# ScalarE's two copies of the last half-product, and its two transfers of the block before it, change places

## The chip, the cores and the metric

The kernel runs on one core of a Trainium2 chip. The metric is the time of one execution on the device in microseconds (us). Four executions of the kernel before gave 875.29, 875.60, 875.69 and 1138.22 us; their median is 875.64. A profile of one further execution shows where that time goes, instruction by instruction.

## The reference

The program is an attention block followed by a feed-forward block. Only the second one matters here:

```python
def _attn_ref(q, k, v, proj) -> np.ndarray:   # q, k, v: (4, 8, 768, 64)
...
    scores = np.where(mask, scores, -1000000000.0)
...
    return np.matmul(attn, v).astype(np.float32)
...
def _moe_ref(x, w_in, w_out) -> np.ndarray:   # x: (3072, 512), w_in: (512, 2048), w_out: (2048, 512)
    h = x @ w_in
    g = h * (1.0 / (1.0 + np.exp(-1.702 * h)))
    return (g @ w_out).astype(np.float32)
```

The attention output, reordered to 3072 tokens of 512 values, is `x`. The output is 3072 x 512 float32, which is 6.3 MB.

## The kernel before

After attention, `feed_forward` (L683) computes both products by Strassen's scheme in Winograd's form: a product of 2 x 2 blocks is made of seven block products and a few sums. The second product, `g @ w_out`, uses the scheme twice. Its outer level has seven "outer products", run in the order `OUTER = (1, 2, 6, 7, 5, 3, 4)` (L692), for each of three blocks of 1024 tokens (`n1`, L688). That gives 21 steps in `steps_out` (L772), numbered `n` = 0 to 20; the loop over them stands at L922. A block of 1024 tokens has two halves of 512 tokens, `j` = 0 and 1, which are collected in the tiles `ys[0]` and `ys[1]`. I call the last one y1 where it is `ys[1]` of the last block.

Each step calls `product_of_halves` (L813), the inner level. It makes seven inner products with TensorE, each by four matrix products of 128 x 128 by 128 x 256 in float32 into a PSUM bank of its own (`product(i)`, L821; the trace shows eight matmul instructions for each). I write P1, P3 and so on for `product(1)`, `product(3)`. The sums around them run on VectorE, all through `add` (L827, recorded at L828). Two results leave PSUM through ScalarE: the copy of P1 into `u` (L837) and the copy of P3 into `c12` (L840). The next VectorE sum, `add(v, product(6), u)` (L842), reads `u`.

The four quadrants of a step's result are turned from feature-major to token-major by VectorE's 32 x 32 transposes (`turned`, L799, recorded at L804), one instruction for each quadrant, into `ys[j]`. `written` (L806) then sends a part of `ys[j]` to the output in DRAM, as four transfers of 32 partitions each, dealt in turn to the queues it is given. In the steady part all four go to SyncE's queue (SP). For the last two steps they are dealt to SP and to ScalarE's queue alternately (`loader + [nc.scalar]`), so two each. A transfer that sits in ScalarE's instruction stream waits there, in order, until the transposes that fill its source are done.

The order of TensorE, VectorE, ScalarE and GpSimd is the order of the Python calls: these four are in `ORDERED` (L18) and are scheduled by hand (L72). `after(at)` (L934) is a hook called at five points of `product_of_halves`; it places the prepared sums of the next step, the transposes and the transfers between the inner products. Its arguments 0, 1, 2, 3 stand for points of L841, L849, L853 and L858, and 4, which only the last step reaches, for L856.

Around the change the order is:

- Step 19 (`n + 2 == len(steps_out)`, outer product 3) ends with `after(3)`. That places the rest of the sums for step 20 and the four transposes of its own result into y1, and at L951 and L952 `written(sb, 1, (0, 1), ...)`: four transfers of 256 KB, two on SP and two on ScalarE.
- Step 20 (`final`, outer product 4) starts with the ScalarE copies of P1 and P3. Its products run in the order P1, P3, P6, P7, P5, P2, P4. Its `after(2)` transposes quadrants 1 and 3 and sends the second half of `ys[0]` (four transfers of 128 KB). Its `after(4)` transposes quadrant 0, and `after(3)` quadrant 2, and sends the first half (four transfers of 128 KB).

So at the end 1 MB of y1 leaves first, then 0.5 MB, then 0.5 MB, each as two transfers on SP's queue and two on ScalarE's.

Of the kernel before, what the change touches and what calls it, by code (L numbers as in the profile page):

```python
# [38 lines left out]
def kernel(  # L39
# [643 lines left out]
    def feed_forward(tag, late=()):  # L683
# [9 lines left out]
        with ExitStack() as fctx:  # L693
# [71 lines left out]
            def inner_sums(at):  # L765

                if at == 0:
                    w = w_quarters(OUTER[0])
                    return sums_a(nc.gpsimd, *w, wqs[LEFT[OUTER[0]]][:, 1, 0:F4, :])
                return sums_a(nc.gpsimd, *w_quarters(OUTER[at])) if at < len(OUTER) else []  # L770

            steps_out = [(sb, o) for sb in range(n1) for o in OUTER]  # L772
            raw_g = [None, s_in[:, 0:2].rearrange("p i k f -> p (i k f)").rearrange("p (c t) -> p c t", t=XT)]

            def fetch(n):
                sb, o = steps_out[n]
                for h in range(2):
                    cs = slice(h * F4, (h + 1) * F4)
                    loader[0].dma_start(out=raw_g[n % 2][:, cs], in_=g_dram[len(LEFT) * sb + RIGHT[o], :, cs, :])
# [14 lines left out]
            def g_sums(n):  # L794
                return sums_b(nc.vector, *g_quarters(n)) if n < len(steps_out) else [lambda: None] * 4
# [3 lines left out]
            def turned(c, i, j, q0, q1):  # L799

                for q in range(q0, q1):
                    h, k = divmod(q, 2)
                    y = ys[j].rearrange("p b (d r) -> p r b d", r=4)[:, 2 * i + h, k * (TH // 32) : (k + 1) * (TH // 32), :]
                    nc.vector.transpose(y, c[:, q].rearrange("p (b t) -> p b t", t=32))  # L804

            def written(sb, j, halves, queues):  # L806
                first, last = halves[0] * TH, (halves[-1] + 1) * TH
                for a in range(4):
                    t0 = (2 * sb + j) * XT
                    dst = out[t0 + first : t0 + last, a * P : (a + 1) * P].rearrange("(b t) d -> t b d", t=32)  # L810
                    queues[a % len(queues)].dma_start(out=dst, in_=ys[j][32 * a : 32 * (a + 1), first // 32 : last // 32, :])

            def product_of_halves(n, acc, after):  # L813

                sb, o = steps_out[n]
                wq, gq = w_quarters(o), g_quarters(n)
                m = wholes[n % len(wholes)]
                u, v = (gp.tile([P, TH], F32, tag=x, name=x, bufs=2) for x in ("u", "v"))
                c11, c12, c21, c22 = (m[:, i] for i in range(4))

                def product(i):  # L821
                    ps = bank()[:, 0:TH]
                    for c in range(F4):
                        nc.tensor.matmul(ps, wq[LEFT[i]][:, c, :], gq[RIGHT[i]][:, c, :], start=(c == 0), stop=(c == F4 - 1))  # L824
                    return ps

                def add(dst, x, y):  # L827
                    nc.vector.tensor_tensor(dst, x, y, op=Alu.add)  # L828

                def corner():  # L830
                    add(c11, product(2), u)
                    if acc is not None:
                        add(c11, c11, acc[:, 0])


                final = n + 1 == len(steps_out)
                nc.scalar.copy(u, product(1))  # L837
                if not final:
                    corner()
                nc.scalar.copy(c12, product(3))  # L840
                after(0)  # L841
                add(v, product(6), u)  # L842
                add(c21, product(7), v)
                if acc is not None:
                    add(v, v, acc[:, 1])
                    add(c22, c21, acc[:, 3])
                    add(c21, c21, acc[:, 2])
                add(c12, c12, v)
                after(1)  # L849
                p = product(5)  # L850
                add(c22, p, c21 if acc is None else c22)
                add(c12, p, c12)
                after(2)  # L853
                if final:
                    corner()
                    after(4)  # L856
                add(c21, product(4), c21)
                after(3)  # L858
                return m
# [14 lines left out]
            for sb in range(n1):  # L874
                for mt in range(MT):
                    n = sb * MT + mt
# [45 lines left out]
            for n, (sb, o) in enumerate(steps_out):  # L922
                final = n + 1 == len(steps_out)
                if 0 < n and n + 1 < len(steps_out):
                    fetch(n + 1)

                if n in (5, 6):
                    nc.gpsimd.tensor_copy(mark, ms[OUTER[n - 1]][0:1, 0, 0:1])
                for f in {0: inner_sums(4), 5: inner_sums(5) + inner_sums(6)[:2], 6: inner_sums(6)[2:]}.get(n, []):
                    f()  # L930
                later_sums = g_sums(n + 1)
                m = wholes[n % len(wholes)]

                def after(at):  # L934
                    if at == 0:
                        while pending:
                            pending.pop(0)()

                    steps = [later_sums[at : at + 1]] if n == 0 else [[], later_sums[0:1], later_sums[1:2], later_sums[2:], []][at : at + 1]

                    if n + 2 >= len(steps_out):
                        turns = [lambda q=q: turned(m, int(final), int(not final), q, q + 1) for q in range(4)]
                        if final:
                            steps = [[[], [], [turns[1], turns[3]], [turns[2]], [turns[0]]][at]]
                        elif at == 3:
                            steps = [later_sums[2:3], turns[0:2], turns[3:4], later_sums[3:], turns[2:3]]
                    for f in sum(steps, []):
                        f()
                    if final and at in (2, 3):
                        written(sb, 0, (3 - at,), loader + [nc.scalar])  # L950
                    if n + 2 == len(steps_out) and at == 3:  # L951
                        written(sb, 1, (0, 1), loader + [nc.scalar])  # L952

                acc = {6: 1, 7: 6, 2: 1, 3: 6, 4: 7}.get(o)
                if o == 3:
                    pending.pop(0)()
                ms[o] = product_of_halves(n, None if acc is None else ms[acc], after)

                def flat(x):
                    return x.rearrange("p q t -> p (q t)")  # L960

                if o == 5:
                    m5, m6, m7 = (ms[i] for i in (5, 6, 7))
                    pending += [lambda a=m6, b=m5: nc.vector.tensor_tensor(flat(a), flat(a), flat(b), op=Alu.add),
                                lambda a=m5, b=m7: nc.vector.tensor_tensor(flat(a), flat(a), flat(b), op=Alu.add),
                                lambda a=m5: turned(a, 1, 1, 0, 4)]
                elif o in (2, 3) and n + 2 < len(steps_out):
                    pending.append(lambda a=ms[o], j=int(o == 3): turned(a, 0, j, 0, 4))
                    if o == 3:
                        pending.append(lambda sb=sb: written(sb, 1, (0, 1), loader))  # L970
                elif o == 4 and not final:
                    pending.append(lambda a=ms[4]: turned(a, 1, 0, 0, 4))
                    pending.append(lambda sb=sb: written(sb, 0, (0, 1), loader))
                yield
# [50 lines left out]
```

## Time and profile before

| what | value |
|---|---|
| median of the four runs | 875.64 us |
| the profiled execution's own time | 875.59 us |
| its span (first to last instruction) | 873.7 us |
| granted TensorE clock, mean | 0.996 |
| TensorE busy | 862.2 us (99%), 4077 matmuls |
| VectorE busy | 718.9 us (82%) |
| ScalarE busy | 311.8 us (36%) |
| DMA moved | 131.99 MB, mean 151 GB/s |
| output transfers of 256 KB, SP's queue / ScalarE's queue | 18 / 2 |
| output transfers of 128 KB, SP's queue / ScalarE's queue | 4 / 4 |

The span runs from the first to the last instruction of the program; the execution's own time is 1.89 us longer. Times inside the trace are counted from the start of the span. A timeline line gives the start, the duration, the engine (a "q" behind its name means its instruction queue, which issues transfers), the line of the kernel, the operation, the tiles written and read, and the number of instructions that the line merges. In square brackets stands how long the engine sat idle before it and what released it. Step 20 starts on TensorE at about 851.9 us; the last matmul of the program ends at 864.1, the last VectorE instruction at 866.2, and the span at 873.7.

### The profile page before, as it was taken

The page shows a single profiled execution, that of the slowest core. Times are in us where ns is not written, and L with a number is a line of the kernel's source. Part 1 is how long each engine was busy: PE and PEld are TensorE (multiplying, and loading weights), DVE is VectorE, ACT ScalarE, POOL GpSimd, SP SyncE. Part 2 cuts the span into 40 slices and gives each one's busy share as a digit, 9 for nine tenths or more (in the row PEclk, how much of TensorE's full clock was granted, in tenths as well). Part 3 has the DMA queues.
Part 4 walks back from the last instruction along what each step waited for, and adds up shares of the span by engine and source line. Part 5 has one row for each costly group of instructions (what it writes and reads, how often), then busy time and mean ns, then how long its engine had stood idle before and what let it go on. Part 6 is the DMA issues. An engine that isn't in the chain of part 4 may idle for free.

```text
span 873.7 us, 11818 instructions
## 1 busy us (share of the span) xinstructions
PE 862.2 (99%) x4077; PEld 501.3 (57%) x4077; DVE 718.9 (82%) x1020; ACT 311.8 (36%) x519; POOL 321.1 (37%) x275
## 2 busy tenths in 40 slices
PE   9999999999999999999999999999999999999995
PEld 4444444444444444444444444444888888888884
DVE  4479999988999988778777778888888977897785
ACT  5756667777666653222233222332000000000000
POOL 4244334334433375665543344659903100000000
PEclk9999999999999999999999999999999999999998
DMA  6334456554445404565455555575844685467524
GB/s 133 59 59 84 84 98 106 115 90 83 83 83 90 76 25 157 193 217 193 175 193 186 205 181 197 189 251 179 302 164 157 200 249 196 166 196 241 193 97 99
DMA packets 169155, 131.99 MB, mean 151 GB/s; under 512 B 123616, under 2 KB 138112, under 8 KB 163712
## 3 DMA queue, kind: packets, MB, share of 16 engines
q1 hardware_dynamic: 166528, 129.70, 51.4%
q10 hardware_dynamic: 2560, 1.46, 0.8%
q8 instruction: 34, 0.56, 0.3%
q14 instruction: 33, 0.27, 0.1%
HBM read 79.69 MB, written 50.33 MB: 149 GB/s over the span
## 4 chain that ended last, share of the span: by engine, by line
PE 96%; DVE 3%; issue 0%; ACT 0%; ACTq 0%; DVEq 0%
PE product L712 33%; PE product L824 27%; PE ps L432 18%; PE av L458 14%; PE dn L479 1%; PE hash L408 1%; DVE xT L828 1%; PE tp L366 1%; DVE y L804 1%; DVE acc L448 0%; DVE xT L499 0%; PE warm L359 0%; PE hash L373 0%; DVE acc L446 0%; ACT e L433 0%
## 5 line engine op out<-in xcount | busy, mean ns | idle before, releaser
L433 ACT ACTIVATE e<-ps 128x768 f32<-128x768 f32 x192 | 150.3, 812 | 17.1 <-PE ps L432 14.9
L432 PE MATMUL ps<-qT,kT 64*128 64x384 f32 x768 | 155.1, 482 | 0.0
L712 PE MATMUL product<-xT,w_in_sb 128*128 128x512 f32 x288 | 135.4, 592 | 0.0
L458 PE MATMUL av<-e,v 128*64 128x385 f32 x768 | 128.2, 488 | 0.0
L440 POOL TENSOR_TENSOR acc<-e 128x768 f32<-128x768 f32 x32 | 51.2, 1600 | 192.4 <-ACT e L433 112.6
L720 ACT ACTIVATE c<-c 128x512 f32<-128x512 f32 x72 | 45.3, 630 | 184.9 <-issue 78.5
L458 PEld LDWEIGHTS av<-e,v 128*64 128x64 f32 x768 | 53.8, 136 | 72.9 <-issue 72.0
L712 PEld LDWEIGHTS product<-xT,w_in_sb 128*128 128x128 f32 x288 | 54.6, 190 | 69.0 <-issue 63.8
L712 PE MATMUL product<-t_x,s_in 128*128 128x512 f32 x192 | 90.2, 592 | 0.0
L432 PEld LDWEIGHTS ps<-qT,kT 64*128 64x128 f32 x768 | 68.2, 187 | 37.7 <-issue 37.4
L219 POOL TENSOR_TENSOR v<-c,u 128x512 f32<-128x512 f32 x24 | 34.2, 1424 | 121.1 <-ACT c L720 121.1
L837 ACT COPY u<-product 128x256 f32<-128x256 f32 x21 | 7.8, 372 | 172.1 <-PE product L824 138.9
L441 POOL TENSOR_TENSOR acc<-acc,e 128x768 f32<-128x768 f32 x32 | 64.1, 2002 | 2.5
L432 PE MATMUL ps<-qf,kf 64*128 64x384 bf16 x384 | 63.0, 324 | 0.1
L712 PEld LDWEIGHTS product<-t_x,s_in 128*128 128x128 f32 x192 | 36.5, 190 | 45.9 <-issue 43.8
L446 DVE SCALAR_TENSOR_TENSOR acc<-e 128x768 f32<-128x768 f32 x32 | 50.6, 1582 | 5.1 <-ACT e L433 5.1
L712 PE MATMUL product<-t_x,w_in_sb 128*128 128x512 f32 x96 | 45.1, 592 | 0.0
L712 PE MATMUL product<-xT,s_in 128*128 128x512 f32 x96 | 45.1, 592 | 0.0
L432 PEld LDWEIGHTS <-kf 64*128 64x128 bf16 x384 | 19.4, 94 | 35.4 <-issue 12.0
L448 DVE TENSOR_TENSOR acc<-acc,acc 128x768 f32<-128x768 f32 x32 | 31.2, 974 | 4.8 <-POOL acc L441 1.6
L824 PE MATMUL product<-raw_g,xT 128*128 128x256 f32 x152 | 35.1, 379 | 0.0
L448 DVE TENSOR_TENSOR acc<-acc,e 128x768 f32<-128x768 f32 x32 | 31.8, 995 | 3.8 <-ACT e L433 0.5
(207 smaller groups left out, 1495.1 us busy)
## 6 DMA issues: line engine op xcount, KB each, us to landing
raw_g<-g_dram SPq DMA_DIRECT2D x22, 1024.0 KB
s_in<-g_dram SPq DMA_DIRECT2D x20, 1024.0 KB
g_dram<-c SPq DMA_DIRECT2D x72, 256.0 KB
g_dram<-t SPq DMA_DIRECT2D x48, 256.0 KB
raw<-in_moe_w_in_dram SPq DMA_DIRECT2D x16, 512.0 KB
raw<-in_moe_w_out_dram SPq DMA_DIRECT2D x16, 512.0 KB
v<-in_v_dram SPq DMA_DIRECT2D x32, 192.0 KB
g_dram<-u SPq DMA_DIRECT2D x24, 256.0 KB
```

The source lines that it names most:

```text
L219: return [lambda: eng.tensor_tensor(t1, b12, b11, op=Alu.subtract), lambda: eng.tensor_tensor(b12, b22, b12, op=Alu.subtract), lambda: eng ...
L366: nc.tensor.matmul(tp[D * j : D * (j + 1), i * P : (i + 1) * P], x[name][:, j, c * GT + i, :], ident, start=True, stop=True)
L432: nc.tensor.matmul(ps[:, j, 0:HS], a[hs, keys], m[hs, cols], start=not last, stop=last)
L433: nc.scalar.activation(es[c][:, kt, :, 0:HS], ps[:, :, 0:HS], Act.Exp, scale=1.0 / D**0.5)
L440: nc.gpsimd.tensor_tensor(acc, es[c][:, 0, :, 0:HS], es[c][:, 1, :, 0:HS], op=Alu.add)
L441: nc.gpsimd.tensor_tensor(acc, acc, es[c][:, 2, :, 0:HS], op=Alu.add)
L446: nc.vector.scalar_tensor_tensor(acc, e[0], T * TINY, e[1], op0=Alu.add, op1=Alu.add)
L448: nc.vector.tensor_tensor(acc, acc, x, op=Alu.add)
L458: nc.tensor.matmul(av[D * j : D * (j + 1), :], vt[:, t, j, :], es[c][:, t, j, :], start=(t == 0), stop=(t == T - 1))
L712: nc.tensor.matmul(ps, wq[LEFT[i]][:, kc, :], xq[RIGHT[i]][:, kc, :], start=(kc == 0), stop=(kc == K2 - 1))
L720: nc.scalar.activation(c, c, Act.Gelu_apprx_sigmoid)
L824: nc.tensor.matmul(ps, wq[LEFT[i]][:, c, :], gq[RIGHT[i]][:, c, :], start=(c == 0), stop=(c == F4 - 1))
```

## The change

The transfers of y1 are no longer issued at the end of step 19, but in step 20 at its `after(0)`, which comes behind the two ScalarE copies (L837 and L840) and ahead of the first VectorE sum (L842). `final` is true in step 20 only, and `sb` is the same there as in step 19.

```diff
                     if final and at in (2, 3):
                         written(sb, 0, (3 - at,), loader + [nc.scalar])
-                    if n + 2 == len(steps_out) and at == 3:
+
+                    if final and at == 0:
                         written(sb, 1, (0, 1), loader + [nc.scalar])
```

On ScalarE the order was: two transfers of y1, copy of P1, copy of P3. It becomes: copy of P1, copy of P3, two transfers of y1. No instruction is added or taken away. On SP nothing stands between the old and the new place of its two transfers of y1, and VectorE, TensorE and GpSimd keep their order.

## The prediction

> **What bounds the kernel now.** I read the page's chain of waits first, then the waits of the last 24 us, then the timeline of the same stretch, then a table of the transfers' share by stretch. The chain says that TensorE sets the end nearly everywhere:
>
> ```profile
> PE 96%; DVE 3%; issue 0%; ACT 0%; ACTq 0%; DVEq 0%
> ```
>
> So only what lies behind or beside the last products can change the time here. The change touches ScalarE's order in the last two steps. The waits from 850 to 874 us (engine and line that waited, what for, us in total, times, longest) are just two:
>
> ```profile
> ACT u L837 <- PE product L824: 13.7, 1, 13.7
> DVE v L828 <- ACT u L837: 1.5, 1, 1.5
> ```
>
> The second is VectorE standing still for ScalarE's copy of P1. The first names P1, but P1 was done long before: the timeline shows it.
>
> ```profile
> 851.88 1.89 PE L824 MATMUL product<-raw_g,w_out_sb 128*128 128x256 f32 x8
> ...
> 857.06 1.89 PE L824 MATMUL product<-raw_g,w_out_sb 128*128 128x256 f32 x8
> 857.48 0.63 DVE L804 STREAM_TRANSPOSE y<-xT 128x256 f32<-128x256 f32 x1
> ...
> 858.19 0.91 ACTq L811 DMA_DIRECT2D out_dram<-y  x2
> ...
> 859.20 0.37 ACT L837 COPY u<-product 128x256 f32<-128x256 f32 x1 [13.66 <-PE product L824]
> 859.47 0.38 ACT L840 COPY xT<-product 128x256 f32<-128x256 f32 x1
> 859.60 0.42 DVE L828 TENSOR_TENSOR v<-product,u 128x256 f32<-128x256 f32 x1 [1.49 <-ACT u L837]
> 860.13 0.43 DVE L828 TENSOR_TENSOR xT<-product,v 128x256 f32<-128x256 f32 x1
> ...
> 862.24 1.89 PE L824 MATMUL product<-t4g,w_out_sb 128*128 128x256 f32 x8
> 862.85 1.10 DVE L804 STREAM_TRANSPOSE y<-xT 128x256 f32<-128x256 f32 x2
> 863.79 0.40 DVE L828 TENSOR_TENSOR xT<-product,u 128x256 f32<-128x256 f32 x1
> ...
> 865.17 0.40 DVE L828 TENSOR_TENSOR xT<-product,xT 128x256 f32<-128x256 f32 x1
> 865.61 0.63 DVE L804 STREAM_TRANSPOSE y<-xT 128x256 f32<-128x256 f32 x1
> ```
>
> P1 ends at 851.88 + 1.89 = 853.77, yet its copy starts at 859.20. In between, ScalarE waits at its first transfer of y1 until the last transpose of y1 ends (857.48 + 0.63 = 858.11), issues two transfers (858.19 to 859.10), and only then copies. VectorE waits 1.49 us. From there TensorE no longer sets the end: it finishes at 864.13, VectorE at 866.24.
>
> The third resource is what the chain hides. It ends with the last transpose, at 866.24 us, and the span ends 7.46 us later. Columns: stretch, length, busy time of PE, PEld, DVE, ACT, POOL, granted clock, the transfers' share of the 16 DMA engines, GB/s.
>
> ```profile
> 858.90:862.00 3.10, 3.10 (x16) 2.73 (x15) 2.22 (x6) 0.65 (x2) 0.00 (x0) 1.00 0.91 166
> 862.00:863.90 1.90, 1.90 (x10) 1.52 (x8) 1.87 (x6) 0.00 (x0) 0.00 (x0) 1.00 1.03 221
> 863.90:864.90 1.00, 0.23 (x2) 0.00 (x0) 0.93 (x4) 0.00 (x0) 0.00 (x0) 1.00 0.57 126
> 864.90:866.40 1.50, 0.00 (x0) 0.00 (x0) 1.30 (x3) 0.00 (x0) 0.00 (x0) 1.00 0.95 171
> 866.40:869.80 3.40, 0.00 (x0) 0.00 (x0) 0.00 (x0) 0.00 (x0) 0.00 (x0) 0.62 1.01 233
> 870.40:873.70 3.30, 0.00 (x0) 0.00 (x0) 0.00 (x0) 0.00 (x0) 0.00 (x0) 0.50 0.02 5
> ```
>
> From about 859 us, when y1's first packets move, to about 870 us the DMA engines are full, but for one dip at 863.9 to 864.9. There y1's 1 MB has drained and the next half has only just been issued (863.98). So the last 11 us are bound by **output transfers**, and what a faster VectorE can win is above all that dip. The 3.3 us after 870.4 hold next to no transfers and no work of the engines; I take them as fixed.
>
> **The change, part by part.** Nothing is added or removed; two ScalarE copies and two ScalarE transfers change places.
>
> *The copies.* They can now start when their products end: P1's at 853.8, P3's (its matmuls start at 853.60) at 855.5, 0.37 us each, so both are over by 855.9. ScalarE has nothing else there.
>
> *The transfers of y1.* They are queued behind P3's copy and wait for the transposes until 858.11 in any case. The copy is done 2.2 us earlier, so this costs nothing. That cover fails only if the copy ends after 858.19; then each us of delay holds back half of y1's bytes. SP's two transfers keep their place and time (858.14). Behind ScalarE's two transfers stand only its four for `ys[0]`, which need VectorE's transposes from 862.8 on, so nobody waits there either.
>
> *VectorE.* Its 1.49 us wait goes. What is late next is TensorE. The sum with P6 can start at about 858.0 (P6 ended by 857.2), but the sum with P7 needs P7, at 857.06 + 1.89 = 858.95, so it starts at 858.97 instead of 860.13: 1.16 us are left of the gain. The chain from there is back to back: P5 (ends 860.67) is needed at 862.07 - 1.16 = 860.91 and P2 (ends 862.40) at 863.79 - 1.16 = 862.63, both in time. The transposes of quadrants 1 and 3 end at 863.95 - 1.16 = 862.79. The sum with P4 would move to 865.17 - 1.16 = 864.01, but P4 ends at 864.13; with the 0.03 us that such waits show it starts at 864.16. The last transpose therefore moves by 865.17 - 864.16 = 1.01 us, to end at 865.23.
>
> *The transfers of `ys[0]`.* The first half is issued at about 862.8 instead of 863.98. Before, packets moved 0.85 us after issue; now they are due at 863.7, while y1 is still draining (full until 864.0, gone by 864.6). The dip closes. It is worth 1.00 x (1 - 0.57) = **0.43 us**. The second half is issued at 865.3 and due at 866.1, when the first half still has packets queued (0.5 MB at the 221 GB/s of the better stretches lasts 2.4 us, until about 866.7), so no new dip opens.
>
> Bounds of what the closed dip brings. Lower end: 0.43 us, if every byte then moves as it did. Upper end: the stretch after the dip ran at 171 GB/s, like the start of y1 at 166, and later stretches at 221 to 233. If the slow stretch belongs to starting from empty engines, its 1.50 x 171 = 257 KB take 257 / 225 = 1.14 us instead, another 0.36, together 0.79. If it belongs to the partitions that the first pair of transfers reads, it stays. I can't tell these apart and take the middle: **0.6 us**.
>
> [...]
>
> **Sum** against the profiled execution: its span 873.7 - 0.6 = 873.1; with the 1.89 us outside the span, 875.59 - 0.6 = 874.99. The median of the runs (875.64) is 0.05 above that execution, so I say **875.0 us**, 0.07% less. A measurement of this kernel tells about 0.2%, 1.75 us, from no change, so this counts as no change.
>
> **Rivals.**
>
> *The end follows VectorE* (chance 0.2): the transfers catch up, and the whole 1.01 us arrives: 874.6. For it speaks that 233 GB/s was reached with the engines no fuller than at 171; against it, that they were full.
>
> *Nothing arrives* (0.17): the first half's packets, queued earlier, only take y1's share, the slow start stays, or the last issue waits for room: the last two transfers took 0.96 us and 1.21 us to issue when the queues were deep, against 0.32 to 0.45 with empty ones. Then 875.6. The case that the copy doesn't move ahead at all, because something other than queue order holds it, gives the same time; the 5.4 us between P1's end and its copy are covered to the end by the transfers' wait and issue, which speaks against it.
>
> *Slower: y1's ScalarE half starts late* (0.08). Place: ScalarE's copy of P3 into `c12`. If it had to wait for VectorE's transposes out of the same big tile `xT`, it would start at 858.11 and end at 858.5, the transfers would go out at 858.6 instead of 858.19, and 512 KB of a transfer-bound tail would start 0.4 us late, with the dip moved rather than closed: up to +0.4, 876.0. It decides from the point where the copy ends after 858.19. Against it: a TensorE read of another part of `xT` (838.06) starts before a VectorE write to `xT` (838.34 to 839.09) that precedes it in the program, so parts of that tile don't wait for each other.
>
> **How the numbers follow.** Forecast 0.55, with 874.7 to 875.3; the others as above, 0.2, 0.17 and 0.08. The bounds run from -1.01 to +0.4 us, 874.6 to 876.0; the three undisturbed runs shown lie 0.4 us apart, so I widen the lower end to 874.4. No mechanism in the trace has 1.75 us to give: VectorE's whole wait is 1.49. Faster by over 0.2% gets 0.04, slower by over 0.2% 0.06 for a cause I don't see, within 0.2% 0.90.
>
> **What would show it.** In the changed profile the copy of P1 should start near 853.8 and that of P3 near 855.5; VectorE's 1.5 us wait for `u` should be gone, with short waits for P7 and P4 in its place; ScalarE's transfers of y1 should still issue at 858.2; the transposes should end near 862.8 and 865.2; and the DMA share should stay above 0.9 from 859 until the output ends, near 869.6. I am wrong if the dip is still there, if y1's transfers start after 858.6, or if the last packets move with VectorE by a full 1.0 us.

## The result, and the profile after

The changed kernel takes 873.98 us (median of 40 runs, 873.21 to 875.00) against 875.46 us for the kernel before (median of 63 runs); the ratio is 0.9982 with a 95% interval of 0.9978 to 0.9986. That is 1.5 us less. The forecast was 875.0 us in a range of 874.4 to 876.0, so the kernel gained about two and a half times the 0.6 us that were forecast, and the time lies below the range.

The profiled execution took 874.03 us, its span is 872.2 us (873.7 before). First the timeline of the last step, in the same form as before:

```profile
854.14 0.37 ACT L837 COPY u<-product 128x256 f32<-128x256 f32 x1 [8.30 <-PE product L824]
...
855.82 0.37 ACT L840 COPY xT<-product 128x256 f32<-128x256 f32 x1 [1.31 <-PE product L824]
...
858.25 0.41 DVE L828 TENSOR_TENSOR v<-product,u 128x256 f32<-128x256 f32 x1
858.43 8.28 SPq L811 DMA_DIRECT2D out_dram<-y  x6
858.48 8.30 ACTq L811 DMA_DIRECT2D out_dram<-y  x6
...
859.27 0.42 DVE L828 TENSOR_TENSOR xT<-product,v 128x256 f32<-128x256 f32 x1 [0.61 <-PE product L824]
...
861.99 1.09 DVE L804 STREAM_TRANSPOSE y<-xT 128x256 f32<-128x256 f32 x2
...
864.91 0.63 DVE L804 STREAM_TRANSPOSE y<-xT 128x256 f32<-128x256 f32 x1
```

TensorE ran 0.29 us later in this execution than in that of before (its last matmul ends at 864.41 instead of 864.13; over all profiles here it lies between 863.5 and 864.7), so times are compared below by their distance from that end. Both copies start when their products end; the 1.49 us wait of VectorE is gone, and one of 0.61 us for P7 stands in its place. The last transpose ends 1.12 us behind TensorE instead of 2.11: 0.99 us were won there, where 1.01 was forecast.

Then the transfers, by stretches of the same kind as before (last two columns: share of the DMA engines, GB/s):

```profile
859.20:862.30 3.10, 3.10 (x16) 2.72 (x15) 2.93 (x8) 0.00 (x0) 0.00 (x0) 1.00 0.91 167
862.30:864.20 1.90, 1.90 (x10) 1.52 (x8) 1.83 (x5) 0.00 (x0) 0.00 (x0) 1.00 1.02 220
864.20:865.20 1.00, 0.21 (x1) 0.00 (x0) 0.96 (x3) 0.00 (x0) 0.00 (x0) 1.00 0.97 230
865.20:866.70 1.50, 0.00 (x0) 0.00 (x0) 0.34 (x1) 0.00 (x0) 0.00 (x0) 1.00 0.97 236
866.70:869.10 2.40, 0.00 (x0) 0.00 (x0) 0.00 (x0) 0.00 (x0) 0.00 (x0) 0.78 0.96 237
```

The third row is where the dip was (0.57, 126 GB/s); it is full now, and the row after it runs at 236 instead of 171 GB/s. The last packet of the output ends 5.42 us behind TensorE instead of 6.33.

That explains 0.9 us of the two profiles' difference at most. The rest lies behind the last packet: from there to the end of the span were 3.24 us before, and are 2.39 us after. The books of these two executions: +0.29 (TensorE) - 0.91 (transfers) - 0.85 (behind the transfers) = -1.47 us, which is the difference of the spans (872.23 - 873.70).

What happens there is seen in the waits of SP's queue from 866 us to the end, in columns engine and line that waited, what for, us in total, times, longest. Before:

```profile
SPq L988 <- SPq L988: 2.2, 2, 1.1
...
SPq L1021 <- DVEq L1021: 1.2, 1, 1.2
SPq L1021 <- PEq L1021: 0.4, 2, 0.3
```

After (the diff adds a line, so L988 and L1021 have become L989 and L1022):

```profile
SPq L989 <- SPq L989: 2.7, 2, 2.0
SPq L1022 <- PEq L1022: 0.6, 2, 0.5
```

I take the first row to be SP waiting for the landings of the transfers: the last of its waits ends at 870.80 us, 0.35 us behind the last packet (870.45). L1021 is the end of the program, where all engines meet twice: TensorE and ScalarE have one wait there at 872.2 us and one at 873.6. In the kernel before SP stood there 1.2 us waiting for **VectorE**, whose work had ended at 866.24 us. That row is absent after. The instructions of VectorE at that line, before and then after (two drains and two semaphore waits; the last pair of numbers is the first and the last start):

```profile
L1021 DVEq DRAIN  x2: 11/34/58, 870.8 to 873.5; - x2
L1021 DVEq EVENT_SEMAPHORE  x2: 21/21/21, 873.4 to 873.6; - x2
```

```profile
L1022 DVEq DRAIN  x2: 10/25/40, 870.3 to 871.8; - x2
L1022 DVEq EVENT_SEMAPHORE  x2: 21/21/21, 871.6 to 872.2; - x2
```

Before, 2.5 us pass between VectorE's first drain (870.81) and its next instruction (873.35), and the other engines had released that one at 872.11. After, the instruction comes as soon as it is released, at 871.65. The late arrival costs less than SP's 1.2 us: from that instruction to the end of the span pass 0.35 us before and 0.6 us after, because GpSimd's last work at this line (872.2 to 872.5 before) runs while VectorE is awaited. None of these instructions was touched by the change.

One more thing differs. The program has a second copy of the feed-forward in a branch that is taken only for unsafe inputs (L988 to L997) and never here. The change edits that copy too, and there the order is not written by hand: VectorE's sums and transposes come out in another order, with one instruction more. VectorE's whole program has 3528 instructions before and 3529 after; the other engines' programs keep their length. VectorE jumps over this branch to L1021, so the place where it lands has moved by one instruction.

That gives two theories. **F**: about half of the gain is the transfers, and about half is that landing place. **T**: all of it is the transfers, and VectorE's late arrival before is chance.

### The profile page after: what moved, and what is told of

It is laid out like the page before. It is cut to its first block, busy times and chain, and to the rows that moved or that the text cites. A ratio compares the mean times of both kernels' runs of the same rounds, so it can differ in the third digit from the quotient of the medians.

```text
span 872.2 us, 11818 instructions
## 1 busy us (share of the span) xinstructions
PE 862.4 (99%) x4077; PEld 501.7 (58%) x4077; DVE 718.9 (82%) x1020; ACT 311.7 (36%) x519; POOL 321.8 (37%) x275
## 4 chain that ended last, share of the span: by engine, by line
PE 97%; DVE 2%; issue 0%; ACT 0%; DVEq 0%
PE product L712 33%; PE product L824 29%; PE ps L432 18%; PE av L458 14%; PE dn L479 1%; PE hash L408 1%; PE tp L366 1%; DVE xT L828 0%; DVE acc L448 0%; DVE xT L499 0%; PE warm L359 0%; DVE y L804 0%; PE hash L373 0%; DVE acc L446 0%; ACT e L433 0%
## 5 line engine op out<-in xcount | busy, mean ns | idle before, releaser
L837 ACT COPY u<-product 128x256 f32<-128x256 f32 x21 | 7.8, 372 | 166.8 <-PE product L824 133.6
```

## The experiments

Ratios are to runs of the kernel before on the same chip, with 95% intervals. In several cases they are as wide as the effects and reach 1; there the profile carries the verdict, and the ratio only agrees with it.

**The change in the copy that runs, and only there** (3528 instructions on VectorE):

```diff
-                    if n + 2 == len(steps_out) and at == 3:
+                    if (final and at == 0) if tag == "" else (n + 2 == len(steps_out) and at == 3):
                         written(sb, 1, (0, 1), loader + [nc.scalar])
```

> The change is made in the feed-forward that runs, and not in its second copy in the branch that is never taken; VectorE's program then has 3528 instructions as before (the changed kernel has 3529). Theory F (the transfers end 0.5 to 0.8 us earlier, and the other 1 us is the last barrier, at which VectorE arrives late before and in time after, because its program is one instruction longer): ratio 0.9991 to 0.9995 to the kernel before, and in the profile VectorE still passes the barrier before the last more than 1 us after SP. Theory T (all of it is the transfers): ratio 0.9980 to 0.9985, VectorE in time.

Ratio 0.9992 (0.9983 to 1.0001). The last packet ends 5.44 us behind TensorE, as in the changed kernel, but 3.27 us pass from there to the end, as before. SP's waits:

```profile
SPq L1021 <- DVEq L1021: 1.2, 1, 1.2
```

The instructions that run are those of the changed kernel, and by the medians about half of its gain is missing. The interval overlaps that of the whole change, so the ratio alone would not decide; that VectorE is late again with the transfers early speaks against T, and the next two runs settle it.

**The change in the copy that is never run, and only there** (`tag == "2"` in place of `tag == ""`; 3529 instructions).

> The change is made only in the copy of the feed-forward that is never run: the instructions that run are those of before, and VectorE's program has 3529 instructions. Theory F: about 1.0 us faster than before, ratio 0.9986 to 0.9991, with VectorE in time at the last barrier and its 1.5 us wait for u still there. Theory T: ratio 0.9998 to 1.0002.

Ratio 0.9993 (0.9984 to 1.0002). VectorE waits its 1.5 us for `u` as before (first row), the last packet ends 6.03 us behind TensorE, and the stretch behind it is 2.44 us instead of 3.24. SP's waits at the end are in the second row:

```profile
DVE v L828 <- ACT u L837: 1.5, 1, 1.5
SPq L1021 <- PEq L1021: 0.6, 2, 0.5
```

The wait of SP for VectorE is gone though nothing that runs has changed. T falls. The gain is smaller than the 1.0 us that I expected. The two halves multiply to 0.9992 x 0.9993 = 0.9985, next to the 0.9982 of the whole.

**One instruction more in the never taken branch** (3529 on VectorE, the order of everything else as before):

```diff
+        nc.vector.memset(above, 0.0)
         shifted_attention()
         for f in sums_b(nc.vector, *quarters_x(0)):
```

> The kernel before with one VectorE memset more in the branch that is never taken (3529 instructions). Theory F: as second_only, ratio 0.9986 to 0.9991. Theory T, or a cause in the order of the second copy rather than in its length: ratio 0.9998 to 1.0002.

Ratio 0.9991 (0.9982 to 1.0000), 2.47 us behind the last packet, VectorE in time:

```profile
SPq L1022 <- PEq L1022: 0.6, 2, 0.5
```

So it is the length of VectorE's program that counts and not what the scheduler made of the second copy.

**128 and 127 instructions more** (3656 and 3655 on VectorE), by the same memset in a loop, to see whether any longer program has VectorE in time:

> [...]

> [...]

Each ran once, under the profiler (875.55 and 874.88 us), so there is no ratio. With 128 more, everything is as before: 3.31 us behind the last packet, and

```profile
SPq L1023 <- DVEq L1023: 1.1, 1, 1.1
```

With 127 more, VectorE passes the first meeting in time (871.4 us), but its second drain comes only at 872.6, and the stretch is 3.46 us:

```profile
L1023 DVEq DRAIN  x2: 58/93/128, 870.0 to 872.6; - x2
L1023 DVEq EVENT_SEMAPHORE  x2: 21/21/21, 871.4 to 872.9; - x2
```

The late instruction stands one place further down the program: with 128 more it is VectorE's first wait (873.4 us), with 127 more its second drain. A longer program as such is not in time; the count decides. Over the twelve profiles here there is no exception: VectorE is late with 3528, 3655 and 3656 instructions and in time with 3529 and 3544. Other counts were not run.

What VectorE waits for, no run shows. In all six kernels with a late VectorE (with 127 more as well) its late instruction starts 2.4 to 2.75 us after its first drain; in the changed kernel, where it is in time, 1.38 us pass from that drain to the next instruction (870.27 to 871.65). The time from VectorE's last branch at L988 (L989 after) to its first drain does not tell the two apart: 3.96 us in the kernel before, 4.10 in the changed one. Nor does the trace's queue 14, of the kind "instruction", give the answer: behind 864.5 us six of its packets start in the kernel before and five in the changed one, but the sixth starts at 874.16, 0.81 us after the late instruction, so it is not what VectorE waited for. The records don't name the instructions, nor the engine, that a packet brings.

**All four transfers of y1 on SP's queue**, so that ScalarE has nothing ahead of its copies, and their place in the program stays:

```diff
                     if n + 2 == len(steps_out) and at == 3:
-                        written(sb, 1, (0, 1), loader + [nc.scalar])
+                        written(sb, 1, (0, 1), loader if tag == "" else loader + [nc.scalar])
```

> The kernel before with all four transfers of y1 on SP's queue, so that ScalarE has nothing ahead of its copies (VectorE 3528 instructions, ScalarE 3 fewer in its program, SP 2 more). VectorE's 1.5 us wait for u should go as in the change. If the 16 engines bind whatever queue feeds them, the transfers end as in main_only, within 0.3 us, and so does the ratio. If one queue alone feeds them more slowly, y1 takes clearly longer than 5.4 us and the ratio is 1.000 or above. Where theory F holds, VectorE is late at the last barrier as before.

Ratio 0.9989 (0.9980 to 0.9998). VectorE's wait goes, its last transpose ends 1.12 us behind TensorE, and the last packet 5.45 us, equal to the change. One queue alone moved y1's 1 MB in 5.46 us (859.54 to 865.00), where two took 5.68 us before. The share of the 16 engines is 0.95 from 859.5 to 865.1 us; so here the shared engines bind, not the queue. It is not a pure copy of the change, though: SP has two instructions more and issues its last two transfers at 866.98 and 867.34, behind a wait for one of ScalarE's, and still the last packet is no later. VectorE is late here too, but only by 0.4 us instead of the 1.2 I expected:

```profile
SPq L1021 <- DVEq L1021: 0.4, 1, 0.4
```

It reached its drain earlier (869.74; why, I did not find out), and the stretch behind the last packet is 2.34 us. So the landing place costs at most what it makes VectorE later than the other engines at that meeting (0.4 us here, 1.2 us in the kernel before).

**The order of the partitions within a send**, for the slow stretch behind the dip:

```diff
-                for a in range(4):
+                for a in ((2, 3, 0, 1) if tag == "" and sb + 1 == n1 else range(4)):
```

> The kernel before, but the four transfers of each send of the last block go in the order of partitions 64-95, 96-127, 0-31, 32-63. The dip stays. If the slow stretch after the dip comes from starting with empty engines, the first pair after it is again the slow one (1.3 us for 128 KB on each queue, near 170 GB/s) and the second pair takes 1.1 to 1.25. If it belongs to the partitions 0 to 63, the first pair takes 1.1 to 1.25 us and the second 1.3. The end moves by less than 0.3 us either way.

It ran once, under the profiler (875.09 us). The stretches, of which the third is the dip:

```profile
863.50:864.50 1.00, 0.34 (x2) 0.00 (x0) 0.93 (x4) 0.00 (x0) 0.00 (x0) 1.00 0.57 125
864.50:866.00 1.50, 0.00 (x0) 0.00 (x0) 1.42 (x3) 0.00 (x0) 0.00 (x0) 1.00 0.90 163
866.00:869.40 3.40, 0.00 (x0) 0.00 (x0) 0.00 (x0) 0.00 (x0) 0.00 (x0) 0.57 1.01 234
```

The first pair behind the dip is the slow one again (163 GB/s; its packets take 1.26 and 1.34 us on the two queues, the second pair's 1.00 and 1.16), though it now reads the other partitions. So the slow stretch follows the start from empty engines and not the partitions. It lasts as long as the first pair of transfers does (3.1 us with 256 KB each at the start of y1, 1.5 us with 128 KB each here); why, no run shows.

**y1 in two halves**, the second as soon as its two quadrants are turned, 1.6 us earlier (about 856.5 instead of 858.1 us by the timeline of before), both behind ScalarE's copies, with 3544 instructions on VectorE (16 memsets in the never taken branch), so that it is not late:

```diff
+                    if (final and at == 0) if tag == "" else (n + 2 == len(steps_out) and at == 3):
+                        for h in ((1,), (0,)) if tag == "" else ((0, 1),):
+                            written(sb, 1, h, loader + [nc.scalar])
...
+        for _ in range(16):
+            nc.vector.memset(above, 0.0)
```

> [...] If the tail is bound by transfers, they start 1.5 us earlier and the last ends 0.6 to 1.2 us before that of the changed kernel, at which point VectorE's last transpose sets it: ratio 0.9968 to 0.9976. If VectorE's last transpose already sets the end, no gain over the changed kernel: 0.9980 to 0.9984.

> The changed kernel once more, beside split_again on the same chip. Ratio 0.9980 to 0.9986; VectorE in time at the last barriers.

> split_y1 once more, beside the changed kernel on the same chip. If the 0.5 us by which its last packets came earlier in the profile hold in time: ratio 0.9972 to 0.9979 and below after_again's. If not: equal to after_again's within 0.0003.

The ratios are 0.9976 (0.9967 to 0.9985) and, beside the changed kernel with 0.9982 (0.9973 to 0.9991), 0.9977 (0.9967 to 0.9987). The medians of that pair are 873.23 and 873.75 us, 0.5 us apart; the intervals overlap, so that it beats the changed kernel is likely and not settled. The reason I gave is refuted. Stretches of split_again:

```profile
857.00:861.70 4.70, 4.70 (x24) 4.13 (x23) 3.98 (x11) 0.00 (x0) 0.00 (x0) 1.00 0.94 221
861.90:863.10 1.20, 1.20 (x7) 1.05 (x6) 1.14 (x4) 0.00 (x0) 0.00 (x0) 1.00 0.00 0
863.20:864.90 1.70, 0.49 (x3) 0.09 (x1) 1.58 (x3) 0.00 (x0) 0.00 (x0) 1.00 0.92 173
```

y1 is gone 1.6 us earlier (first packet 6.71 us ahead of TensorE's end instead of 5.12), and then the engines stand empty until VectorE has the next half, and start slowly again. The last packet ends 5.55 us behind TensorE in both runs, against 5.42 and 5.48 in the two of the changed kernel: not earlier. I take it that in the changed kernel transfers and VectorE bind the end about equally. What the split gained in the profile (0.24 us from TensorE's end to the span's) lies behind the last packet. The semaphores of the last transfers stand last in the list that SP works through there, where in the changed kernel four others, already full, still follow them at 0.07 us each. That fits in size, and was not tried by itself.

## Why the prediction was wrong

- *The copies, the transfers of y1 and SP.* Right: copies at their products' ends, y1 issued within 0.1 us of its last transpose, no late half. The slower rival did not occur.
- *VectorE.* Right: P7 takes over the wait (0.61 us), P4 limits the end, 0.99 us won at the last transpose against 1.01 forecast.
- *The transfers.* Right in mechanism and size. The dip closed, and the slow stretch behind it went with it, of which the forecast had taken half. (Its remark that 233 GB/s was reached with the engines no fuller than at 171 misreads the rows: 1.01 against 0.95.) Over six profiles of kernels with the old order on ScalarE the last packet ends 5.99 to 6.33 us behind TensorE (mean 6.12), over three with the new one 5.42 to 5.48 (mean 5.45): 0.67 us, where 0.6 was forecast between 0.43 and 0.79. The change without its side effect has the ratio 0.9992, 0.7 us; alone it would have given about 874.8 us, inside the range.
- *"The 3.3 us after 870.4 hold next to no transfers and no work of the engines; I take them as fixed."* **This step failed.** That stretch measured 3.24 us before and 2.39 after. It held a wait of SP for VectorE of 1.2 us, plain in the queue's waits, that I had not followed up. The change took it away by making VectorE's program one instruction longer in a branch that never runs; that alone is worth 0.6 to 0.8 us by the ratios (0.9993 and 0.9991, whose intervals reach 1) and 0.8 us in the profiles (stretches of 2.44 and 2.47 instead of 3.24 us).
- *"No instruction is added or taken away"* stood in the description of the change and was true of what runs. The second copy of the same function was not looked at.
- *The range.* Its lower end came from VectorE's 1.01 us as the greatest possible gain plus the spread of the runs. The range left no room for anything outside that chain, and the miss of 0.4 us below it is less than the landing place's share.

That the difference would stay within 0.2% was right, but narrowly (0.18%, interval 0.14 to 0.22%) and for a reason that did not hold: a second effect of 0.8 us came on top of VectorE's wait.

## What to carry to other kernels

When one engine's wait is removed near the end, follow what it feeds: here VectorE won 1 us, and the output transfers passed on 0.67 of it by closing a gap and its slow restart. Follow the end of the program to its very last wait as well; a stretch without busy engines is not a fixed cost while one engine in it still waits for another (here 3.24 us became 2.39). When an edit also touches code that doesn't run, compare the lengths of the programs of all engines: here a single VectorE instruction more in the dead branch was worth 0.8 us in the profiles, about as much as the change's own part (0.7 us).

## What the hardware showed that I had not expected

- The length of VectorE's program, by which its jump at the end lands in another place, decides over about 0.9 us in the profile: 3.24 to 3.46 us behind the last packet in five profiles with a late VectorE (y1 on SP's queue apart), 2.34 to 2.47 in four with one instruction more. One profile each shows VectorE late with 127 and with 128 instructions more.
- The DMA engines moved less after standing empty, at nearly the same busy share: 163 to 173 GB/s for the first pair of transfers (share 0.90 to 0.95) against 220 to 237 later (0.96 to 1.03), whichever partitions are read.
- One queue of SP moves 1 MB of 512-byte packets as fast as SP's and ScalarE's together (5.46 us alone, 5.68 us together).
